# Block-sparse attention and a gated MLP on one core: the output product in one piece, and the end of the kernel in another order

## The chip, the core and the metric

The kernel runs on one core of one Trainium2 chip. That core has a matrix engine (PE in the profile, with its weight loads shown as PEld), three engines for elementwise work (DVE, ACT and POOL) and a queue that mainly issues transfers (SP). They run side by side and wait for each other through semaphores. The metric is the device time of one execution in microseconds (us); lower is better.

## The reference: what is computed

Two stages follow each other. The first is attention over 4 batches, 8 heads, 768 positions and a head size of 64, with a mask made of 32 x 32 blocks (a band of three blocks, the first and last block row and column, and three sampled blocks for each block row). The second is a small MLP over the 3072 rows of 512 that come out of it:

```
scores = scale * q @ k.T ; scores = where(mask, scores, -1e9)
attn   = softmax(scores) ; x = attn @ v            # rows of 512
h      = x @ w_in                                  # 512 -> 1024
solu   = h * softmax(h)
ln     = (solu - mean(solu)) / sqrt(var(solu) + 1e-6) * g_ln
out    = ln @ w_out                                # 1024 -> 512
```

## The kernel before, in words

**Passes and units.** The 24 groups of 128 query rows are taken two at a time, in 12 passes; a pass covers 256 query rows of one batch and all 8 heads. A pass has 12 units (`SLOTS`): 4 pairs of heads times 3 groups of 256 keys. For each unit, `scores` (line 407) issues four matmuls into a PSUM tile `sco`, of which there are two; `exps` (423) is one ACT instruction over 128 x 1024 elements that reads it and so frees it; `outs` (431) issues eight small matmuls into `op`. The unit after next can therefore write its scores only when this unit's `exps` is through. After the third unit of a pair, DVE normalises into the tile `xb`.

**The layer.** Each pass leaves two tiles of 128 rows for the MLP, worked on during the next passes, in between the units. Of one tile: a transfer transposes `xb` into `xT`; `h_mms` (482) issues eight matmuls into `h` (one buffer); `e_exp` (491) is one ACT instruction, `e`, with the row sums; `solu` (499) is one DVE product, after which `h` is free; `ln_turn` sends `solu` through a transposing transfer into `lnT`; `stats` (516) and `rstd` (524) are two and three DVE instructions and a small one on POOL; `o_mms` (542) issues eight matmuls from `lnT` into `o`; `scaled` (550) multiplies by `rstd`, and `store` sends the result out. The softmax's sum and the mean are folded into the statistics and into centred weights `w_cen_sb`.

**What sets the order.** The order is written out by hand. `at(when, fn, ...)` puts a step into a list with a due time in units; `emit` (293) sorts the list by due time and calls the steps, so each engine gets its instructions in this order, and nothing is reordered later. `layer` (815) enters one tile's steps with the due times that its callers give; the tiles of the passes 0 to 9 go through it, twenty in all. For them the eight matmuls of `o` stand in two places: seven at 0.84 of a unit, the eighth at 1.83, which is behind the next unit's four score matmuls (due at 0.8 of each unit) and, for the last of the twenty, also behind the sixteen `outs` matmuls that follow these there. The next tile's first two `h` matmuls come right after the eighth.

**The end.** The last two passes are entered apart. The last pass's first three quarters of `xT` come by transfers; its last quarter is transposed on PE by `x_last` (858) and copied by ACT. `h_end` (868) issues the last two tiles' `h` matmuls into score buffers (`he` in the profile), in four steps over `c`, for two halves each. From `end` on, a list (line 943 on) gives the order: `e_exp`, `solu`, `stats` and `rstd` of the two last tiles (pass `LP`) and of the tile before them; the second tile's `o` of the pass before (`o_mms` with `LP - 1, 1`, whose `lnT` comes by a transfer); PE transposes `ln_mm` (879) into `ln_tp`, copied to `lnTe` by ACT (`ln_out`, 887); `o` of the first last tile (`oe`); and `o` of the second last tile in two halves (`o_half`, `oe1a` and `oe1b`), scaled by DVE and by ACT (`scale_half`), each half with a store of its own.

**The flags.** `check_r`, `check_e`, `check_sum` and `check_bad` (925 to 939) test on DVE that the sums of the softmaxes are in range, add up the flags (`n_ok`), compare the sum (`bad`), and bring the result through a one-column matmul into `bad_i`. All engines read `bad_i` and branch on it; with every flag set, as here, they go on to the end.

Of the kernel before, what the change touches and what calls it, by code (L numbers as in the profile page):

```python
# [208 lines left out]
def kernel(  # L209
# [24 lines left out]
    KD = d_model // 128  # L234
    KF = d_ff // 128
# [6 lines left out]
    PC = 2  # L242
# [5 lines left out]
    SLOTS = NP * UP  # L248
# [6 lines left out]
    n_r, n_e = NPASS * NP * 4, n_tiles  # L255
# [28 lines left out]
    p_op = work.enter_context(tc.tile_pool(name="p_op", bufs=1, space=bass.MemoryType.PSUM))  # L284
# [5 lines left out]
    def at(when, fn, *args):  # L290
        plan.append((when, len(plan), fn, args))

    def emit():
        for _, _, fn, args in sorted(plan, key=lambda x: x[:2]):
            fn(*args)
        plan.clear()
# [98 lines left out]
    def unit(s):  # L395
        ps, r = divmod(s, SLOTS)
        pr, u = divmod(r, UP)
        b, j = divmod(ps, NPB)
        return ps, b, j, pr, u
# [174 lines left out]
    with tc.manual_schedule():  # L574
# [198 lines left out]
        for s in range(n_units):  # L773
            ps, b, j, pr, u = unit(s)
# [37 lines left out]
                at(t0 + t_s, shift, b, pr, key, PC if pr == NP - 1 else 0)  # L812


        def layer(ps, i, hs, es, os):
            for when, n0, n1 in hs:
                at(when, h_mms, ps, i, n0, n1)
            at(es, e_exp, ps, i)
            head = ps == 0 and i == 0
            at(es + (0.33 if head else 0.5), solu, ps, i)  # L820
            at(es + 0.55, ln_turn, ps, i)
            at(es + (6.6 if head else 3.4 if ps == 0 else 2.45 if i == 0 else 1.7), stats, ps, i)
            at(es + (6.7 if head else 3.5), rstd, ps, i)
            for when, n0, n1 in os:
                at(when, o_mms, ps, i, n0, n1)
            out_at = 29.87 if head else os[-1][0] + 0.1
            at(out_at, scaled, ps, i, nc.vector)
            at(out_at + (2.2 if i == PC - 1 and ps < NPASS - 3 else 0.02), store, ps, i)

        LP = NPASS - 1  # L830
        for ps in range(LP):
            b0 = SLOTS * (ps + 1)
            if ps == 0:
                at(b0 + 2.4, x_first, ps)
            else:
                at(b0 - 0.1, x_turn, ps, 0, KD)
            if ps == LP - 1:
                break
            for i in range(PC):
                hs = b0 + 6 * i  # L840
                os = hs + (12 if ps == LP - 2 and i == PC - 1 else 14)
                layer(ps, i,
                      [(hs + 3.9, 0, 2), (hs + 4.85, 2, 3), (hs + 5.86, 3, 5), (hs + 6.85, 5, 7),
                       (hs + (7.79 if hs == SLOTS else 7.85), 7, 8)], hs + 8.5, [(os + 0.84, 0, 7), (os + 1.83, 7, 8)])


        ps, b0 = LP - 1, SLOTS * LP
# [67 lines left out]
        def tile_in(pool, tag, name):  # L915
            if pool is p_sco:
                return lambda: p_sco.tile([128, 2, HF], FP32, tag=tag, name=name)[:, 0, :]
            return lambda: pool.tile([128, d_model], FP32, tag=tag, name=name)
# [11 lines left out]

        def check_sum():
            nc.vector.reduce_sum(out=n_ok[:, 0:1], in_=okr, axis=AX.X)
            nc.vector.tensor_scalar(out=bad, in0=n_ok[:, 0:1], scalar1=float(n_r + n_e),
                                    scalar2=None, op0=ALU.is_lt)

        def check_bad():
            bad_ps = p_h.tile([1, 1], FP32, tag="h", name="bad_ps")
            nc.tensor.matmul(bad_ps, bad, ones_c, start=True, stop=True)
            nc.vector.tensor_copy(out=bad_i, in_=bad_ps)

        end = SLOTS * NPASS
        A, V = nc.scalar, nc.vector
        for n, (fn, *args) in enumerate((
            (h_end, 0, 2, KD),
            (e_exp, LP, 0),
            (o_mms, LP - 1, 0, 5, 8),
            (scaled, LP - 1, 0, A),
            (store, LP - 1, 0),
            (stats, LP - 1, 1),
            (rstd, LP - 1, 1),  # L950
            (check_r, n_r - 2 * PC, n_r),
            (h_end, 1, 0, KD),
            (solu, LP, 0),
            (stats, LP, 0),
            (e_exp, LP, 1),
            (o_mms, LP - 1, 1, 0, 3, tile_in(p_op, "op", "o_10")),
            (ln_mm, 0),
            (ln_out, 0, A),
            (o_mms, LP - 1, 1, 3, 8),
            (solu, LP, 1),  # L960
            (rstd, LP, 0),
            (stats, LP, 1),
            (o_mms, LP, 0, 0, 2, tile_in(p_sco, "sco", "oe0")),
            (ln_mm, 1),
            (ln_out, 1, A),
            (rstd, LP, 1),
            (check_e,),
            (o_mms, LP, 0, 2, 8),
            (scaled, LP - 1, 1, A),
            (store, LP - 1, 1),  # L970
            (scaled, LP, 0, A),
            (store, LP, 0),
            (o_half, 0, p_sco, "sco"),
            (o_half, 1, p_op, "op"),
            (scale_half, 0, V, nc.sync),
            (check_sum,),
            (check_bad,),
            (scale_half, 1, A, nc.scalar),
        )):
            at(end + 0.01 * n, fn, *args)  # L980
# [3 lines left out]
        at(end - 1.12, h_end, 0, 0, 2, (1,))  # L984
        at(end - 1.0, x_last)
        at(end - 1.9, check_r, 0, n_r - 2 * PC)
        at(end - 1.05, o_mms, LP - 1, 0, 0, 3)
        at(end - 0.95, o_mms, LP - 1, 0, 3, 5)
        emit()

    work.close()
# [32 lines left out]
```

## Time and profile before

| what | value |
|---|---|
| time, median of 3 runs | 208.02 us (207.55 to 208.16) |
| the profiled execution's own time | 208.32 us |
| its span, first to last instruction | 206.8 us |
| PE busy over the span | 199.0 us |
| ACT busy over the span | 175.2 us |
| DVE busy over the span | 141.1 us |
| granted PE clock | 1.00 throughout |

All numbers of the trace come from one execution. Times within it count from the span's start. A row of the timeline gives the start, the length, the engine, the line, the operation, output<-input, the shape and the number of like instructions merged into it; brackets give the idle time of that engine ahead of it and what ended it. Matmuls overlap: a row of 512 columns lasts 0.38 us, but the next one starts some 0.215 us after it, so a stop of PE shorter than the difference does not show as idle time.

### The profile page before, as it was taken

Reading aid. Unit: us, or ns where it says so; the run is one execution under the profiler, and the core shown is the slowest. Engines: PE = TensorE matmul, PEld = TensorE weight load, DVE = VectorE, ACT = ScalarE, POOL = GpSimd, SP = SyncE. Lnnn points to the kernel's source line nnn. Section 1 sums busy time; section 2 is a strip of 40 time slices with the busy share of each in tenths; the row PEclk is TensorE's granted clock in tenths of the full one; section 3 lists DMA queues with packets and bytes.
Section 4 is the critical chain, followed back from the end, with each engine's and each line's share of the span. In section 5 each row is a group of like instructions: output and inputs, shape, how many; then the busy total and the mean of one; then the engine's idle time right before and its main releaser. Section 6 shows DMA issues by size and latency. Waiting matters only on the chain.

```text
span 206.8 us, 5603 instructions
## 1 busy us (share of the span) xinstructions
PE 199.0 (96%) x2204; PEld 138.8 (67%) x2238; DVE 141.1 (68%) x331; ACT 175.2 (85%) x209; POOL 110.2 (53%) x167
## 2 busy tenths in 40 slices
PE   7999999999999999999999999999999999999992
PEld 2679967676676676676676676676676676667451
DVE  5688888988755765765665666655665656677982
ACT  6799979889889889889889889879889889897471
POOL 7966799696868274478286273559281110111120
PEclk9999999999999999999999999999999999999999
DMA  5999999979999879999999889999872484556314
GB/s 158 334 367 229 361 373 271 229 134 248 235 264 346 203 168 335 212 153 220 175 232 294 204 161 338 166 241 193 166 196 51 101 105 50 107 125 111 59 50 162
DMA packets 73906, 42.02 MB, mean 203 GB/s; under 512 B 55828, under 2 KB 69396, under 8 KB 73876
## 3 DMA queue, kind: packets, MB, share of 16 engines
q1 hardware_dynamic: 72932, 40.06, 84.1%
q0 software_dynamic: 528, 1.05, 2.7%
q10 hardware_dynamic: 416, 0.52, 0.8%
q8 instruction: 18, 0.29, 0.6%
q14 instruction: 12, 0.10, 0.1%
HBM read 23.07 MB, written 6.29 MB: 142 GB/s over the span
## 4 chain that ended last, share of the span: by engine, by line
PE 90%; DMA 4%; DVE 3%; issue 1%; DVEq 0%
PE sco L416 30%; PE op L444 18%; PE o L547 17%; PE h L487 16%; DMA xT<-xb 3%; PE warm_t L403 2%; DMA lnT<-solu 1%; PE tp_k L346 1%; PE oe L547 1%; PE mean_ps L753 1%; PE tp_q L356 1%; PE he L873 1%; DVE KT L371 1%; DVE QT L664 1%; PE ln_tp L883 0%
## 5 line engine op out<-in xcount | busy, mean ns | idle before, releaser
L427 ACT ACTIVATE exs<-sco 128x1024 bf16<-128x1024 f32 x144 | 141.0, 1024 | 10.3 <-PE sco L416 7.7
L416 PE MATMUL sco<-QT,KT 88*128 88x256 bf16 x576 | 87.4, 274 | 0.3
L416 PEld LDWEIGHTS <-KT 88*128 88x128 bf16 x576 | 54.8, 98 | 31.6 <-issue 4.7
L444 PE MATMUL op<-VA,exs 128*128 128x65 bf16 x1152 | 51.8, 194 | 0.5
L444 PEld LDWEIGHTS <-exs 128*128 128x128 bf16 x1152 | 48.5, 97 | 3.7 <-DVE xb L458 0.3
L487 PE MATMUL h<-w_in_sb,xT 128*128 128x512 bf16 x153 | 48.7, 378 | 0.7
L547 PE MATMUL o<-w_cen_sb,lnT 128*128 128x512 bf16 x166 | 43.3, 379 | 1.0 <-DMA lnT<-solu 0.4
L540 POOL TENSOR_TENSOR rstd<-vpe,mhalf 128x1 f32<-128x1 f32 x24 | 13.2, 549 | 45.4 <-DVE vpe L538 38.9
L457 DVE RECIPROCAL recip_all<-op 128x4 f32<-128x4 f32 x48 | 8.7, 181 | 39.7 <-PE op L444 39.5
L327 POOL COPY KT<-pd 64x768 bf16<-64x768 bf16 (+2 forms) x30 | 21.2, 706 | 23.9 <-DMA pd<-nat 22.8
L496 ACT ACTIVATE e<-h 128x1024 bf16<-128x1024 f32 x22 | 22.5, 1023 | 10.7 <-PE h L487 10.6
L522 DVE BATCH_NORM_STATS2 stats<-solu 128x6 f32<-128x512 bf16 x48 | 30.6, 680 | 0.1
L508 DVE TENSOR_TENSOR solu<-h,e 128x1024 bf16<-128x1024 f32 x22 | 26.7, 1215 | 1.5 <-ACT e L496 1.5
L547 PEld LDWEIGHTS <-lnT 128*128 128x128 bf16 x176 | 15.8, 98 | 14.2 <-DMA lnT<-solu 0.9
L558 DVE TENSOR_SCALAR ot<-o,rstd 128x512 f32<-128x512 f32 x20 | 15.0, 751 | 10.8 <-issue 8.2
L327 POOL COPY QT<-pd 64x768 bf16<-64x768 bf16 (+2 forms) x30 | 20.8, 694 | 1.5
L458 DVE TENSOR_TENSOR xb<-op,recip_all 128x256 bf16<-128x256 f32 x48 | 20.4, 424 | 1.7
L327 POOL CAST nat<-st_q 128x768 bf16<-128x768 f32 (+2 forms) x19 | 13.6, 713 | 14.3 <-DMA st_q<-in_q_dram 14.3
L487 PEld LDWEIGHTS <-xT 128*128 128x128 bf16 x176 | 16.1, 98 | 4.7 <-DMA xT<-xb 0.8
L327 POOL CAST VA<-st_v 128x768 bf16<-128x768 f32 x16 | 13.4, 847 | 1.4 <-DMA st_v<-in_v_dram 0.9
L327 POOL CAST nat<-st_k 128x768 bf16<-128x768 f32 x15 | 12.4, 826 | 3.3 <-DMA st_k<-in_k_dram 3.1
L538 DVE TENSOR_TENSOR vpe<-es,mv 128x1 f32<-128x1 f32 x24 | 6.7, 278 | 0.9
(89 smaller groups left out, 116.5 us busy)
## 6 DMA issues: line engine op xcount, KB each, us to landing
st_v<-in_v_dram SPq DMA_DIRECT2D x16, 384.0 KB, 5.9
out_dram<-ot SPq DMA_DIRECT2D x23, 256.0 KB, 2.8
st_k<-in_k_dram SPq DMA_DIRECT2D x15, 384.0 KB, 5.8
st_q<-in_q_dram SPq DMA_DIRECT2D x12, 384.0 KB, 7.9
w_out_f<-in_moe_w_out_dram SPq DMA_DIRECT2D x4, 512.0 KB, 7.4
st_q<-in_q_dram SPq DMA_DIRECT2D x4, 256.0 KB, 7.9
w_in_sb<-in_moe_w_in_dram POOLq DMA_DIRECT2D x1, 1024.0 KB, 12.0
st_q<-in_q_dram SPq DMA_DIRECT2D x4, 128.0 KB, 4.4
```

The lines of the kernel that those rows point to most:

```text
L327: eng.tensor_copy(out=o, in_=i)
L416: nc.tensor.matmul(sco[:, hh, kk * QW : (kk + 1) * QW], KT[b % 2][0:KR, h * NCH + 2 * u + kk, :], QT[b % 2][0:KR, h * NCH + PC * j : h * N ...
L427: nc.scalar.activation(out=exs_of[ps, pr][:, u].rearrange("p a b c -> p (a b c)"), in_=sco_of.pop(s).rearrange("p a b -> p (a b)"), func=A ...
L444: nc.tensor.matmul(op[:, hh, ic, :], exs[:, u, hh, kk, ic * TQ : (ic + 1) * TQ], VA[b % 2][:, 2 * pr + hh, 2 * u + kk, :], start=(u == 0 a ...
L458: nc.vector.tensor_tensor(out=xb_of[ps][:, pr].rearrange("p c (h d) -> p h c d", h=2), in0=op[:, :, :, 0:D], in1=recip.broadcast_to([TQ, 2 ...
L487: nc.tensor.matmul(h_of[ps, i][:, half, :], xT_of[ps][:, c * PC + i, :], w_in_sb[:, c, half * HF : (half + 1) * HF], start=(c == 0), stop= ...
L496: nc.scalar.activation(out=o, in_=h, func=ACT.Exp, scale=1.0, accum_out=esum_all[:, t : t + 1])
L508: nc.vector.tensor_mul(out=so, in0=h, in1=e)
L522: nc.vector.bn_stats(out=stat_of[ps, i][:, half, :], in_=so[:, half, :])
L540: nc.gpsimd.tensor_tensor(out=rstd_of[ps, i], in0=vpe, in1=mhalf, op=ALU.pow)
L547: nc.tensor.matmul(ops_of[ps, i], lnT_of[ps, i][:, c, :], w_cen_sb[:, c, :], start=(c == 0), stop=(c == KF - 1), skip_group_check=True)
L558: nc.vector.tensor_scalar(out=o, in0=i_, scalar1=r, scalar2=None, op0=ALU.mult)
```

## The change

Four things change. In `layer`, the eight matmuls of `o` are issued in one piece where seven stood; the due time of `scaled` and `store` stays as it was. At the end, the `h` matmuls of both last tiles go ahead of most of the matmuls of `o` of the tile (`LP - 1`, 0), and their two `e` on ACT follow each other directly; of `o` of the tile (`LP - 1`, 1), all eight stand in one piece behind the first transposes. The statistics of the first last tile (`stats`, `LP`, 0) move behind the second `solu`. Of the flags, the last part of `check_r` moves from ahead of the first `solu` to behind the last `rstd`, and the adding-up (`check_sum`) moves ahead of the last tile's scaling, while the comparison stays behind it, in `check_bad`. No instruction is added or taken away: each engine issues as many as before, and POOL and SP issue theirs in the same order.

```diff
--- before.py
+++ after.py
@@ -812,7 +812,7 @@
                 at(t0 + t_s, shift, b, pr, key, PC if pr == NP - 1 else 0)
 
 
-        def layer(ps, i, hs, es, os):
+        def layer(ps, i, hs, es, o_at):
             for when, n0, n1 in hs:
                 at(when, h_mms, ps, i, n0, n1)
             at(es, e_exp, ps, i)
@@ -821,9 +821,8 @@
             at(es + 0.55, ln_turn, ps, i)
             at(es + (6.6 if head else 3.4 if ps == 0 else 2.45 if i == 0 else 1.7), stats, ps, i)
             at(es + (6.7 if head else 3.5), rstd, ps, i)
-            for when, n0, n1 in os:
-                at(when, o_mms, ps, i, n0, n1)
-            out_at = 29.87 if head else os[-1][0] + 0.1
+            at(o_at, o_mms, ps, i, 0, KF)
+            out_at = 29.87 if head else o_at + 1.09
             at(out_at, scaled, ps, i, nc.vector)
             at(out_at + (2.2 if i == PC - 1 and ps < NPASS - 3 else 0.02), store, ps, i)
 
@@ -841,7 +840,7 @@
                 os = hs + (12 if ps == LP - 2 and i == PC - 1 else 14)
                 layer(ps, i,
                       [(hs + 3.9, 0, 2), (hs + 4.85, 2, 3), (hs + 5.86, 3, 5), (hs + 6.85, 5, 7),
-                       (hs + (7.79 if hs == SLOTS else 7.85), 7, 8)], hs + 8.5, [(os + 0.84, 0, 7), (os + 1.83, 7, 8)])
+                       (hs + (7.79 if hs == SLOTS else 7.85), 7, 8)], hs + 8.5, os + 0.84)
 
 
         ps, b0 = LP - 1, SLOTS * LP
@@ -930,10 +929,11 @@
 
         def check_sum():
             nc.vector.reduce_sum(out=n_ok[:, 0:1], in_=okr, axis=AX.X)
+
+        def check_bad():
             nc.vector.tensor_scalar(out=bad, in0=n_ok[:, 0:1], scalar1=float(n_r + n_e),
                                     scalar2=None, op0=ALU.is_lt)
 
-        def check_bad():
             bad_ps = p_h.tile([1, 1], FP32, tag="h", name="bad_ps")
             nc.tensor.matmul(bad_ps, bad, ones_c, start=True, stop=True)
             nc.vector.tensor_copy(out=bad_i, in_=bad_ps)
@@ -941,30 +941,30 @@
         end = SLOTS * NPASS
         A, V = nc.scalar, nc.vector
         for n, (fn, *args) in enumerate((
-            (h_end, 0, 2, KD),
+            (h_end, 0, KD - 1, KD),
             (e_exp, LP, 0),
-            (o_mms, LP - 1, 0, 5, 8),
+            (h_end, 1, 0, KD),
+            (stats, LP - 1, 1),
+            (solu, LP, 0),
+            (rstd, LP - 1, 1),
+            (e_exp, LP, 1),
+            (o_mms, LP - 1, 0, 3, 8),
+            (ln_mm, 0),
+            (ln_out, 0, A),
             (scaled, LP - 1, 0, A),
             (store, LP - 1, 0),
-            (stats, LP - 1, 1),
-            (rstd, LP - 1, 1),
-            (check_r, n_r - 2 * PC, n_r),
-            (h_end, 1, 0, KD),
-            (solu, LP, 0),
+            (solu, LP, 1),
+            (o_mms, LP - 1, 1, 0, 8, tile_in(p_op, "op", "o_10")),
             (stats, LP, 0),
-            (e_exp, LP, 1),
-            (o_mms, LP - 1, 1, 0, 3, tile_in(p_op, "op", "o_10")),
-            (ln_mm, 0),
-            (ln_out, 0, A),
-            (o_mms, LP - 1, 1, 3, 8),
-            (solu, LP, 1),
             (rstd, LP, 0),
             (stats, LP, 1),
             (o_mms, LP, 0, 0, 2, tile_in(p_sco, "sco", "oe0")),
             (ln_mm, 1),
             (ln_out, 1, A),
             (rstd, LP, 1),
+            (check_r, n_r - 2 * PC, n_r),
             (check_e,),
+            (check_sum,),
             (o_mms, LP, 0, 2, 8),
             (scaled, LP - 1, 1, A),
             (store, LP - 1, 1),
@@ -973,7 +973,6 @@
             (o_half, 0, p_sco, "sco"),
             (o_half, 1, p_op, "op"),
             (scale_half, 0, V, nc.sync),
-            (check_sum,),
             (check_bad,),
             (scale_half, 1, A, nc.scalar),
         )):
@@ -984,8 +983,9 @@
         at(end - 1.12, h_end, 0, 0, 2, (1,))
         at(end - 1.0, x_last)
         at(end - 1.9, check_r, 0, n_r - 2 * PC)
-        at(end - 1.05, o_mms, LP - 1, 0, 0, 3)
-        at(end - 0.95, o_mms, LP - 1, 0, 3, 5)
+        at(end - 1.05, o_mms, LP - 1, 0, 0, 2)
+        at(end - 0.95, o_mms, LP - 1, 0, 2, 3)
+        at(end - 0.94, h_end, 0, 2, KD - 1)
         emit()
 
     work.close()
```

## The prediction

> **What bounds the kernel now.** I read the page's busy table and groups first, then the timeline of one layer in the middle, then its first and last counterpart, then the last 17 us. From the page:
>
> ```profile
> span 206.8 us, 5603 instructions
> PE 199.0 (96%) x2204; PEld 138.8 (67%) x2238; DVE 141.1 (68%) x331; ACT 175.2 (85%) x209; POOL 110.2 (53%) x167
> L496 ACT ACTIVATE e<-h 128x1024 bf16<-128x1024 f32 x22 | 22.5, 1023 | 10.7 <-PE h L487 10.6
> ```
>
> PE is busy throughout, and ACT waits for it: 10.6 us in all ahead of `e`. But PE's busy share hides short stops. One layer from the timeline:
>
> ```profile
> 155.00 1.02 ACT L496 ACTIVATE e<-h 128x1024 bf16<-128x1024 f32 x1 [0.57 <-PE h L487]
> 155.49 1.67 PE L547 MATMUL o<-w_cen_sb,lnT 128*128 128x512 bf16 x7
> 156.01 2.84 ACT L427 ACTIVATE exs<-sco 128x1024 bf16<-128x1024 f32 x3
> 156.25 1.22 DVE L508 TENSOR_TENSOR solu<-h,e 128x1024 bf16<-128x1024 f32 x1
> 157.08 0.60 PE L416 MATMUL sco<-QT,KT 88*128 88x256 bf16 x4
> 157.08 0.31 PEld L416 LDWEIGHTS <-KT 88*128 88x128 bf16 x3 [0.19 <-issue]
> 157.51 0.38 PE L547 MATMUL o<-w_cen_sb,lnT 128*128 128x512 bf16 x1
> 157.73 0.59 PE L487 MATMUL h<-w_in_sb,xT 128*128 128x512 bf16 x2
> 158.16 0.49 PE L416 MATMUL sco<-QT,KT 88*128 88x256 bf16 x3
> ```
>
> Seven `o` matmuls last 1.67, one 0.38, so they start (1.67 - 0.38) / 6 = 0.215 apart, and PE is free for the scores at 155.49 + 7 x 0.215 = 157.00. The scores start at 157.08. The first of the three `exs` ends at 156.01 + 1.02 = 157.03: the scores wait for their buffer, which that exponential frees. PE stands still for 0.08 us, hidden under the 0.38 us shown for the last `o`, and the eighth `o`, which needs nothing more, is queued behind the waiting scores. The weight loads show the stop as 0.19 or 0.20 of "issue". It recurs from the first such layer to the last:
>
> ```profile
> 47.20 1.67 PE L547 MATMUL o<-w_cen_sb,lnT 128*128 128x512 bf16 x7
> 48.78 0.31 PEld L416 LDWEIGHTS <-KT 88*128 88x128 bf16 x3 [0.20 <-issue]
> 180.10 0.31 PEld L416 LDWEIGHTS <-KT 88*128 88x128 bf16 x3 [0.20 <-issue]
> ```
>
> At the first, 48.78 - (47.20 + 7 x 0.215) = 0.075. Of the twenty layers 17 have it. The other three are the first (`o` starts late), one whose `lnT` lands late (132.43, below), and the last, where the scores are not held up.
>
> **Part 1, `o` in one piece.** Removed: the stop. The eighth `o` starts at 157.00, the scores at 157.215, past the release at 157.08: nothing is left of it, with 0.13 in reserve. Per layer PE gains 0.075 to 0.08, so 17 x 0.077 = 1.3 us, if nobody else is late next. Behind the moved matmul I look at each in turn.
>
> The `h` pair, by the same spacing, moves to 157.65; it needs `solu`, which ends at 156.25 + 1.22 = 157.47 and releases the weight load 0.05 later. Free. The scores after it move from 158.16 to 158.08; they need the second `exs`, which ends at 156.01 + (2.84 - 1.02)/2 + 1.02 = 157.94: reserve 0.14 less the release, some 0.1. Free, but the tightest. The third `exs` started at 157.82 and now needs scores that end at 157.215 + 0.60 = 157.815: at most 0.05 late, and ACT waits 0.57 for `h` ahead of the next `e`, so the lag dies there. DVE's `scaled` keeps its place and finds `o` done earlier; the store's place in SP's queue is unchanged. No DMA is added.
>
> What can eat some of it is transfers that already land late:
>
> ```profile
> 57.27 0.11 PEld L487 LDWEIGHTS <-xT 128*128 128x128 bf16 x2 [0.29 <-DMA xT<-xb]
> 132.43 1.46 PE L547 MATMUL o<-w_cen_sb,lnT 128*128 128x512 bf16 x6 [0.40 <-DMA lnT<-solu]
> 134.64 0.11 PEld L487 LDWEIGHTS <-xT 128*128 128x128 bf16 x2 [0.49 <-DMA xT<-xb]
> ```
>
> A PE that arrives 0.08 sooner waits 0.08 longer at each of these three, unless their landing moves too. That is 0.24 at most lost, so part 1 lies between -1.3 and -1.06; I take -1.1, near the smaller gain, since the trace does not tell whether these landings follow PE.
>
> **Part 2, the end.** Its rows:
>
> ```profile
> 191.69 0.81 PE L547 MATMUL o<-w_cen_sb,lnT 128*128 128x512 bf16 x3
> 192.34 0.28 PE L861 MATMUL x_tp<-ident,xb 128*128 128x128 bf16 x2
> 192.65 0.37 ACT L864 COPY xT<-x_tp 128x256 bf16<-128x256 bf16 x1 [1.00 <-PE x_tp L861]
> 193.94 1.02 ACT L496 ACTIVATE e<-he 128x1024 bf16<-128x1024 f32 x1 [0.92 <-PE he L873]
> 195.19 1.22 DVE L508 TENSOR_TENSOR solu<-he,e 128x1024 bf16<-128x1024 f32 x1
> 196.32 1.02 ACT L496 ACTIVATE e<-he 128x1024 bf16<-128x1024 f32 x1 [0.68 <-PE he L873]
> 196.40 0.33 PEld L547 LDWEIGHTS <-lnT 128*128 128x128 bf16 x3 [0.61 <-DMA lnT<-solu]
> 197.06 0.61 PE L883 MATMUL ln_tp<-ident,solu 128*128 128x128 bf16 x8
> 197.65 1.21 DVE L508 TENSOR_TENSOR solu<-he,e 128x1024 bf16<-128x1024 f32 x1
> 198.77 0.21 DVE L529 TENSOR_SCALAR es<-esum_all 128x1 f32<-128x1 f32 x1
> 199.20 1.28 DVE L522 BATCH_NORM_STATS2 stats<-solu 128x6 f32<-128x512 bf16 x2
> 199.87 1.01 ACT L325 COPY lnTe<-ln_tp 128x1024 bf16<-128x1024 bf16 x1 [1.14 <-PE ln_tp L883]
> 200.91 0.17 DVE L921 TENSOR_SCALAR okr<-esum_all 128x24 f32<-128x24 f32 x1
> 200.96 1.04 PE L899 MATMUL oe1a<-w_cen_sb,lnTe 128*128 128x256 bf16 x8
> 202.09 0.48 DVE L911 TENSOR_SCALAR ot_last<-oe1a,rstd 128x256 f32<-128x256 f32 x1 [0.80 <-PE oe1a L899]
> 202.49 0.37 DVE L932 TENSOR_REDUCE n_ok<-okr 128x1 f32<-128x216 f32 x1
> 202.90 0.15 DVE L933 TENSOR_SCALAR bad<-n_ok 128x1 f32<-128x1 f32 x1
> 202.96 0.47 ACT L908 ACTIVATE ot_last<-oe1b,rstd 128x256 f32<-128x256 f32 x1 [0.91 <-issue]
> 203.42 0.15 DVE L939 CAST bad_i<-bad_ps 1x1 int32<-1x1 f32 x1 [0.37 <-PE bad_ps L938]
> ```
>
> All in times of before. PE's path: two `o` instead of three stand ahead of `x_tp`, which comes some 0.17 earlier (its `xb` is then the limit), and so does the copy, which ends at 192.85. One `o` and four `he` follow, two `o` fewer than before; the last `he` ends 0.38 sooner, and the first `e` starts at 193.56. The second tile's eight `he` follow without three `o` in between: 0.38 + 3 x 0.215 = 1.03 sooner, `e` at 195.29. The five `o` then run to 196.17; the first `solu` has ended by then (0.23 behind its `e`, as at 156.25, and so by 193.56 + 1.02 + 0.23 + 1.22 = 196.03), so `ln_tp` starts at 196.17 in place of 197.06, and the first `lnTe` copy at 196.82. The eight `o` in one piece start at 196.62, with `lnT` landed by 196.40: the 0.61 of idle weight loads is now filled, with 0.2 to spare. Then two `oe` to 198.78, and the second `ln_tp`, done at 199.39; its copy starts at 199.43 in place of 199.87. All of ACT's and PE's chain behind it is 0.44 earlier: `oe1a` at 200.52, the last ACT scaling at 202.52.
>
> What ACT puts off, the scaling of tile (`LP - 1`, 0), goes between the two copies, where ACT waits 1.14 now; its store goes out later on SP, with only later stores behind it.
>
> DVE's path: the second `solu` follows its `e` by 0.2, at 196.5, 1.15 earlier than before; but the first tile's statistics, which ran while DVE waited for that `e`, now come behind it. Instructions overlap by some 0.08 (`es` starts at 198.77, and the `solu` ahead of it ends at 197.65 + 1.21 = 198.86), so two statistics take 1.28 - 0.08 = 1.20 to their `es`, and `es` to the next step takes 199.20 - 198.77 = 0.43. So: 196.5 + 1.21 - 0.08 = 197.63 statistics, 198.83 `es`, 199.26 statistics, 200.46 `es`, and 200.9 to 200.95 flags, against 200.91. That is the timetable of before: DVE had the time in hand, since it idled 0.80 for `oe1a`. Into this go the moved flags: the two instructions of `check_r`, some 0.3 (twice 0.17 less overlap), `check_e` some 0.4, `n_ok` some 0.3. Scaling starts at about 201.95, not at `oe1a`'s end of 201.56: DVE is the next to be late, by 0.4. Still it is 0.15 ahead of 202.09, and `bad` now follows it directly, without the 0.40 from `n_ok` (202.49) to `bad` (202.90): 0.15 + 0.40 = 0.55 earlier.
>
> The kernel closes after the later of `bad_i` (0.55 earlier) and ACT's last store (0.44 earlier): part 2 is -0.44 to -0.55, and I take -0.5. The moved `rstd` of tile (`LP - 1`, 1) costs nothing: its scaling on ACT comes only behind the second copy. One page of the Trainium skill speaks against this part: "VectorE: DVE Perf Modes", § The DRAIN you can't avoid, has each DVE operation followed by a flush of its duration less 266 ns before the next. By it the two statistics moved behind `solu` would cost 2 x 0.41 more there, and part 2 would come to about +0.2. The rows disagree: `es` starts before `solu` has ended.
>
> **Sum.** -1.1 - 0.5 = -1.6. The profiled execution took 208.32 (1.5 around its span), 0.3 above the median; against the median, 208.02 - 1.6 = 206.4 us, or 206.7 by the profiled one's base.
>
> **The rivals.**
> A. ACT, not PE, sets the pace of the middle: then the gain of part 1 comes back as waits for `exs` a few steps on, and only part 2 is left: 207.5. For it: three `exs` follow each other without a gap, and the next scores have some 0.1 in hand. Against: the 0.57 of ACT's idle time ahead of each `e`. The Trainium skill's "Perfetto Trace Analysis", § Identifying the Most-Contended Engine, would have it so: it takes PE's busy share for no measure, weight loads (67% here) in its place, and occupancy for ACT (85%). 10%.
> B. The middle gains, the end does not: DVE's lengthened queue, or an `lnT` that lands after 196.62, takes part 2 back, between 0 and +0.5: 206.9 to 207.4. For it: DVE is shown above to be the last to come. 13%.
> C. Slower: the scores come 0.13 later behind the longer `o`, and this lag goes round through `exs`, instead of dying at `e`. 17 x 0.13 = 2.2, less part 2: 209.7. It decides if the lag exceeds the 0.57 at `e`; the rows give 0.05. 8%.
> D. The change does nothing that counts: transfers hold PE in the middle (as at 132.43 and 134.64) and closing work hides the end: 208.0. 6%.
> My forecast: 63%.
>
> **Numbers.** Some 0.3%, 0.6 us, is what a measurement of this kernel can tell (its three runs spread over 0.61). The forecast, B and a little of A (which lies at the border, -0.25%) are faster: 0.78. The rest of A and most of D are the same: 0.12. C and the rest of D are slower: 0.10. The range 205.8 to 207.6 holds the forecast, B and A; the forecast's own is 205.8 to 206.9, from all stops gone with 0.6 at the end to three more late landings.
>
> **What would show it.** Right: `sco` rows directly after `o` x8 with no 0.20 "issue" on their weight loads; a layer 0.08 shorter; the last two `e` 1.7 apart, and `ot_last` on DVE waiting for nothing on PE. Wrong: "issue" or ACT waits ahead of the scores that follow the `h` pair (A, C), more time on transposed transfers (D), or a `bad_i` later than 0.4 ahead of before, counted from the tile's last `xb` (B).

## The result, and the profile after

The changed kernel took 206.16 us in the median of six runs (205.58 to 206.53), beside 208.09 for six runs of the kernel before on the same chip: 1.9 us faster by the medians, 1.7 by the ratio of 0.9919 (95% interval 0.9896 to 0.9942, so 1.2 to 2.2 us). The forecast was 206.4. The profiled execution took 205.58, its span 203.94; before it was 208.32 and 206.84.

The page of the changed kernel: the busy shares have hardly moved, and ACT still waits for `h` as long as before.

```profile
PE 195.9 (96%) x2204; PEld 137.3 (67%) x2238; DVE 141.3 (69%) x331; ACT 173.9 (85%) x209; POOL 110.3 (54%) x167
L496 ACT ACTIVATE e<-h 128x1024 bf16<-128x1024 f32 x22 | 22.5, 1023 | 10.7 <-PE h L487 10.6
```

What did move is one row of the groups (line, engine, operation, busy time, mean ns, idle time before it and what ended it): the weight loads of the scores. Before:

```profile
L416 PEld LDWEIGHTS <-KT 88*128 88x128 bf16 x576 | 54.8, 98 | 31.6 <-issue 4.7 <-POOL VA L327 0.7 <-DVE QT L664 0.5
```

After:

```profile
L416 PEld LDWEIGHTS <-KT 88*128 88x128 bf16 x576 | 53.9, 97 | 30.6 <-issue 1.4 <-POOL VA L327 0.7 <-DVE KT L327 0.7
```

The "issue" fell from 4.7 to 1.4 us. In the timeline of the layer that the prediction showed (start, duration, engine, line, operation):

```profile
152.85 1.02 ACT L496 ACTIVATE e<-h 128x1024 bf16<-128x1024 f32 x1 [0.57 <-PE h L487]
153.34 1.89 PE L547 MATMUL o<-w_cen_sb,lnT 128*128 128x512 bf16 x8
153.86 3.80 ACT L427 ACTIVATE exs<-sco 128x1024 bf16<-128x1024 f32 x4
154.85 0.53 PEld L416 LDWEIGHTS <-KT 88*128 88x128 bf16 x4
155.06 0.60 PE L416 MATMUL sco<-QT,KT 88*128 88x256 bf16 x4
155.50 0.60 PE L487 MATMUL h<-w_in_sb,xT 128*128 128x512 bf16 x2
```

Eight `o` from 153.34 at 0.215 end at 155.06, where the scores start; their weight loads wait for nothing. The `h` pair and the next scores (155.94) follow at their spacing (155.50 + 2 x 0.215 = 155.93), four `exs` run without a gap, and `e` still has 0.57 to wait for `h`.

The end of the changed kernel, from the timeline:

```profile
191.12 1.02 ACT L496 ACTIVATE e<-he 128x1024 bf16<-128x1024 f32 x1 [0.71 <-PE he L872]
192.27 1.22 DVE L508 TENSOR_TENSOR solu<-he,e 128x1024 bf16<-128x1024 f32 x1 [0.15 <-ACT e L496]
192.85 1.02 ACT L496 ACTIVATE e<-he 128x1024 bf16<-128x1024 f32 x1 [0.61 <-PE he L872]
193.73 0.61 PE L882 MATMUL ln_tp<-ident,solu 128*128 128x128 bf16 x8
193.76 0.16 DVE L538 TENSOR_TENSOR vpe<-es,mv 128x1 f32<-128x1 f32 x1
193.99 1.23 DVE L508 TENSOR_TENSOR solu<-he,e 128x1024 bf16<-128x1024 f32 x1
195.13 1.28 DVE L522 BATCH_NORM_STATS2 stats<-solu 128x6 f32<-128x512 bf16 x2
198.07 1.04 PE L898 MATMUL oe1a<-w_cen_sb,lnTe 128*128 128x256 bf16 x8
199.17 0.38 DVE L931 TENSOR_REDUCE n_ok<-okr 128x1 f32<-128x216 f32 x1
199.47 0.47 DVE L910 TENSOR_SCALAR ot_last<-oe1a,rstd 128x256 f32<-128x256 f32 x1
199.86 0.14 DVE L934 TENSOR_SCALAR bad<-n_ok 128x1 f32<-128x1 f32 x1
200.07 0.47 ACT L907 ACTIVATE ot_last<-oe1b,rstd 128x256 f32<-128x256 f32 x1 [0.91 <-POOL rstd L540]
200.37 0.14 DVE L939 CAST bad_i<-bad_ps 1x1 int32<-1x1 f32 x1 [0.37 <-PE bad_ps L938]
```

The two last `e` are 1.73 apart, and `ot_last` on DVE waits for nothing on PE: `oe1a` ended at 199.11, DVE came at 199.47. ACT's last scaling starts 0.08 behind the end of `oe1b` (198.95 + 1.04 = 199.99); its row names POOL's `rstd`, which was done 0.8 earlier.

What follows `bad_i` are the engines' reads of it. SP's, before and after, from the view of this tile (line, engine, operation, number; shortest, median and longest in ns; first and last start):

```profile
L992 SPq TENSOR_LOAD <-bad_i x1: 464/464/464, 203.6 to 203.6; - x1
L992 SPq TENSOR_LOAD <-bad_i x1: 612/612/612, 200.5 to 200.5; - x1
```

In all thirteen traces the span ends 2.94 to 2.98 us behind the start of `bad_i`, not counting the length of this read. From the issue of ACT's last store to the end it is anything from 3.22 to 3.46. So it is SP's reading of `bad_i` that the end follows, not ACT's store. `bad_i` came 0.61 earlier, the read took 0.15 longer, and 0.46 is left.

**Where the 2.90 us between the two spans lie.** Executions of one kernel differ in the first 40 us, where the code is the same, so I measure between fixed points: the first weight load of `o` of the third tile, of the nineteenth, and of the twenty-first, which is tile (`LP - 1`, 0). Weight loads of the changed kernel:

```profile
54.18 1.43 PEld L547 LDWEIGHTS <-lnT 128*128 128x128 bf16 x8
176.11 1.43 PEld L547 LDWEIGHTS <-lnT 128*128 128x128 bf16 x8
189.04 0.31 PEld L547 LDWEIGHTS <-lnT 128*128 128x128 bf16 x2
```

The same before:

```profile
54.94 1.21 PEld L547 LDWEIGHTS <-lnT 128*128 128x128 bf16 x7
178.48 1.21 PEld L547 LDWEIGHTS <-lnT 128*128 128x128 bf16 x7
191.48 0.53 PEld L547 LDWEIGHTS <-lnT 128*128 128x128 bf16 x3
```

So 0.76 was there at the third tile, 1.61 came in the sixteen layers up to the nineteenth (123.54 against 121.93), 0.07 in the next two (13.00 against 12.93), and 0.46 behind it (15.36 against 14.90). Not all of the 1.61 is the change: the late `lnT` and `xT` at 132.43 and 134.64 of the profile before are missing here and in the other traces of this study (the one with the changed end alone waits 0.20 for that `xT`, and its layer is no longer than the others). The experiments tell the shares.

### The profile page after: what moved, and what is told of

Read it like the earlier page. It is cut to its first block, busy times and chain, and to the rows that moved or that the text cites. A ratio compares the mean times of both kernels' runs of the same rounds, so it can differ in the third digit from the quotient of the medians.

```text
span 203.9 us, 5603 instructions
## 1 busy us (share of the span) xinstructions
PE 195.9 (96%) x2204; PEld 137.3 (67%) x2238; DVE 141.3 (69%) x331; ACT 173.9 (85%) x209; POOL 110.3 (54%) x167
## 3 DMA queue, kind: packets, MB, share of 16 engines
q0 software_dynamic: 528, 1.05, 2.7%
## 4 chain that ended last, share of the span: by engine, by line
PE 80%; DVE 7%; DMA 4%; POOL 4%; issue 2%; SPq 1%; ACT 0%; DVEq 0%; POOLq 0%
PE sco L416 28%; PE op L444 17%; PE h L487 16%; PE o L547 15%; DMA st_k<-in_k_dram 2%; DVE stats L522 2%; DVE solu L508 2%; DMA lnT<-solu 1%; POOL nat L327 1%; PE mean_ps L753 1%; PE he L872 1%; DVE KT L664 1%; SPq L318 1%; DVE xb L458 1%; DVE vpe L538 1%
## 5 line engine op out<-in xcount | busy, mean ns | idle before, releaser
L416 PEld LDWEIGHTS <-KT 88*128 88x128 bf16 x576 | 53.9, 97 | 30.6 <-issue 1.4
L547 PE MATMUL o<-w_cen_sb,lnT 128*128 128x512 bf16 x166 | 39.9, 379 | 0.5
```

The costliest lines, as they stand in the source:

```text
L416: nc.tensor.matmul(sco[:, hh, kk * QW : (kk + 1) * QW], KT[b % 2][0:KR, h * NCH + 2 * u + kk, :], QT[b % 2][0:KR, h * NCH + PC * j : h * N ...
L547: nc.tensor.matmul(ops_of[ps, i], lnT_of[ps, i][:, c, :], w_cen_sb[:, c, :], start=(c == 0), stop=(c == KF - 1), skip_group_check=True)
```

## The experiments

The table gives, beside the times, the same three distances. "Before" is the median of the kernel before on the same chip.

| kernel | us | before | ratio (95%) | 3rd to 19th `o` | 19th to 21st | 21st to end |
|---|---|---|---|---|---|---|
| before (profile) | | | | 123.54 | 13.00 | 15.36 |
| changed (profile) | 206.16 | 208.09 | 0.9919 (0.9896 to 0.9942) | 121.93 | 12.93 | 14.90 |
| `o` in one piece alone | 206.87 | 207.82 | 0.9962 (0.9940 to 0.9985) | 122.02 | 12.92 | 15.41 |
| the end alone | 207.53 | 207.82 | 0.9988 (0.9959 to 1.0017) | 122.90 | 13.00 | 14.92 |
| `o` as six and two | 211.76 | 207.82 | 1.0206 (1.0156 to 1.0255) | 126.35 | 13.22 | 15.41 |
| one more on ACT | 206.10 | 207.82 | 0.9931 (0.9902 to 0.9959) | 121.82 | 12.92 | 14.92 |
| changed, again | 205.77 | 207.67 | 0.9894 (0.9857 to 0.9931) | 121.89 | 12.93 | 14.90 |
| statistics first | 205.82 | 207.67 | 0.9912 (0.9875 to 0.9948) | 121.85 | 12.93 | 14.75 |
| sum of the flags back | 205.99 | 207.67 | 0.9913 (0.9879 to 0.9947) | 121.87 | 12.93 | 15.00 |
| first `ot` later | 205.84 | 207.67 | 0.9886 (0.9833 to 0.9939) | 121.83 | 12.93 | 14.90 |
| first `rstd` earlier | 204.98 | 207.85 | 0.9856 (0.9815 to 0.9898) | 121.92 | 12.92 | 14.92 |
| that and statistics first | 204.78 | 207.85 | 0.9870 (0.9820 to 0.9920) | 121.99 | 12.92 | 14.77 |
| both, half of the scaling on ACT | 205.03 | 207.85 | 0.9854 (0.9813 to 0.9895) | 121.93 | 12.93 | 14.77 |

### Each part alone

`o` in one piece, with the end of before:

```diff
-                       (hs + ...), 7, 8)], hs + 8.5, [(os + 0.84, 0, 7), (os + 1.83, 7, 8)])
+                       (hs + ...), 7, 8)], hs + 8.5, os + 0.84)
```

> The kernel before with `o` in one piece in every layer, and its own end. My theory (the eighth `o` fills a stop of PE of 0.075 to 0.08 us in 17 layers): 1.1 to 1.3 us faster than before, and the 0.19 to 0.20 of "issue" gone from the weight loads of the scores behind `o`. Rival A (ACT sets the pace) and rival D (nothing counts): within 0.3 us of before. Rival C (the lag goes round): 2.2 us slower. If the 1.9 us between the two kernels came mostly from the end, this run is less than 0.6 us faster.

The changed end, with `o` in seven and one:

```diff
-                       (hs + ...), 7, 8)], hs + 8.5, os + 0.84)
+                       (hs + ...), 7, 8)], hs + 8.5, [(os + 0.84, 0, 7), (os + 1.83, 7, 8)])
```

> The kernel before with the changed end alone, `o` still as seven and one. My theory: 0.4 to 0.6 us faster than before, the first weight load of the last `he` group to the end of the span shorter by that much. Rival B (DVE's lengthened queue or a late `lnT` takes it back): between 0 and 0.5 us slower. If the parts add, the gains of this run and of the one with `o` in one piece together come to the 1.9 us of the whole change, within 0.5.

By the times the first is 0.8 us faster (by the ratio; 0.3 to 1.2), the second 0.25 (from 0.85 faster to 0.35 slower), which by the times alone can't be told from nothing. The fixed points are sharper. Weight loads of `o`, in one piece alone:

```profile
55.29 0.78 PEld L547 LDWEIGHTS <-lnT 128*128 128x128 bf16 x5
177.31 1.43 PEld L547 LDWEIGHTS <-lnT 128*128 128x128 bf16 x8
190.23 0.53 PEld L547 LDWEIGHTS <-lnT 128*128 128x128 bf16 x3
```

and with the changed end alone:

```profile
55.10 0.99 PEld L547 LDWEIGHTS <-lnT 128*128 128x128 bf16 x6
178.00 1.21 PEld L547 LDWEIGHTS <-lnT 128*128 128x128 bf16 x7
191.00 0.31 PEld L547 LDWEIGHTS <-lnT 128*128 128x128 bf16 x2
```

With the end alone, whose middle is that of before, the sixteen layers took 122.90, not 123.54: 0.64 of the profile before belongs to that one execution, most of it to the two late transfers. Against 122.90, `o` in one piece gains 0.88 to 0.97 there, and 0.08 in the next two layers: 1.0 us in all, a little less than the 1.1 to 1.3 expected. The end takes 15.36 to 15.41 with the old order (three traces) and 14.90 to 14.92 with the new (six): 0.46 between the first pair. The parts add, 1.0 + 0.46 = 1.5. Rivals A, C and D of the middle are out, and so is B.

### The stop made larger

```diff
-            [(os + 0.84, 0, 7), (os + 1.83, 7, 8)]
+            [(os + 0.84, 0, 6), (os + 1.83, 6, 8)]
```

> The kernel before with `o` as six and two in place of seven and one, nothing else. My theory: PE then stands still for 0.075 + 0.215 = 0.29 us per layer ahead of the scores, with one more `o` queued behind the waiting scores, so 17 x 0.215 = 3.7 us slower than before, and "issue" of 0.41 on the scores' weight loads. Rival (what the change removes is the cost of breaking off `o`, whatever is left for later): within 0.3 us of before. Rival D (PE is not what sets the pace of the middle): within 0.6 us of before.

4.3 us slower by the ratio (3.2 to 5.3). The layer in the timeline:

```profile
157.14 1.46 PE L547 MATMUL o<-w_cen_sb,lnT 128*128 128x512 bf16 x6
158.73 0.31 PEld L416 LDWEIGHTS <-KT 88*128 88x128 bf16 x3 [0.41 <-issue]
```

"Issue" is 0.41 as worked out ahead, in all layers but the first and the last, and sixteen of them take 126.35 - 122.90 = 3.45 longer, 0.216 each: one matmul of `o`. With the 0.22 of the next two layers that is 3.67, of 3.7 expected. So it is the place of the wait in PE's queue that costs, not breaking off `o`. What of `o` stands behind the waiting scores is paid for in full, until the scores' buffer is free by the time PE gets there.

### Does ACT set the pace?

```diff
+        if ps < NPASS - 1:
+            nc.scalar.activation(out=more, in_=ident, func=ACT.Copy, scale=1.0)
         nc.scalar.activation(out=o, in_=h, func=ACT.Exp, scale=1.0,
```

> The changed kernel with one more instruction on ACT ahead of each `e` of the 22 ordinary tiles (a copy of the 128x128 identity, some 0.25 to 0.3 us, used by nobody). My theory (PE sets the pace, and ACT has 0.57 us of idle time there): within 0.4 us of the changed kernel, so still 1.5 us or more faster than before, and the idle time ahead of `e` down from 10.6 us to about 4. Rival A (ACT sets the pace once the stop is gone): 20 x 0.28 = 5.6 us slower than the changed kernel. If the reserve of 0.1 us of the scores behind the `h` pair is used up in turn: between the two, 1 to 3 us slower.

Its groups on ACT:

```profile
L499 ACT ACTIVATE e<-h 128x1024 bf16<-128x1024 f32 x22 | 22.5, 1022 | 6.8 <-PE h L488 6.8
L498 ACT ACTIVATE more<-ident 128x128 bf16<-128x128 bf16 x22 | 6.7, 306 | 0.0
```

ACT was busy 6.7 us more, and the sixteen layers took 121.82, no longer than without. The wait ahead of `e` fell by 3.8, to 6.8 and not to the 4 expected: instructions on ACT overlap (in the layer at 152 the copy starts at 152.22, 0.09 before the `exs` ahead of it ends, and takes 0.20 of the idle time for its 0.30). Either number is far above the 0 that was paid, so rival A falls. The Trainium skill's rule in "Perfetto Trace Analysis", § Identifying the Most-Contended Engine, which judges PE by its weight loads (67% here) rather than by its 96%, so that ACT's 85% would count for more, does not hold for this kernel.

### What the end is made of

The order on DVE:

```diff
+            (stats, LP, 0),
             (solu, LP, 1),
             (o_mms, LP - 1, 1, 0, 8, tile_in(p_op, "op", "o_10")),
-            (stats, LP, 0),
```

> The changed kernel with the statistics of the last but one tile back ahead of the second `solu`. DVE is busy without a break from 190.8 to 199.9 in the changed kernel, so their place adds nothing to its sum: the second `solu` ends 1.2 later, at about 196.3, just when PE comes to the second `ln_tp` (196.3). Expected: from the last layer's `o` to the end of the span within 0.2 of the 14.9 us of the changed kernel, the second `ln_tp` 0 to 0.15 later. If the order of DVE's work is what made part 2, it goes back towards 15.4.

```profile
193.91 0.16 DVE L538 TENSOR_TENSOR vpe<-es,mv 128x1 f32<-128x1 f32 x1
193.99 1.28 DVE L522 BATCH_NORM_STATS2 stats<-solu 128x6 f32<-128x512 bf16 x2
199.84 0.14 DVE L934 TENSOR_SCALAR bad<-n_ok 128x1 f32<-128x1 f32 x1
```

The end was expected within 0.2, from DVE being busy without a break. It came 0.15 sooner: `bad` comes 10.65 us after the twenty-first `o` (189.19), against 10.82. In the changed kernel the second `solu` starts 0.12 after its `e` (192.85 + 1.02 = 193.87), as the first one does, whose row names ACT; so DVE does stand there, and the expectation was wrong in that: 0.23 from `vpe` (193.76) to `solu`, where it is 0.08 from `vpe` to the statistics in this run. With the statistics ahead this hole is filled. Taken alone, "statistics behind the second solu" therefore costs 0.15 to 0.17. PE's second `ln_tp` stands 7.29 after the twenty-first `o` in both. That the order on PE is what brings the gain follows by elimination, with the sum of the flags (next); neither PE's order nor the new place of `check_r` was changed alone.

The sum of the flags:

```diff
             (check_e,),
-            (check_sum,),
 ...
             (scale_half, 0, V, nc.sync),
+            (check_sum,),
             (check_bad,),
```

> The changed kernel with the sum of the flags back behind DVE's last scaling. By the prediction's step (0.40 from `n_ok` to `bad` saved): `ot_last` on DVE 0.3 earlier, at the end of `oe1a`, `bad` 0.1 to 0.15 later, `bad_i` as much, and the span 0 to 0.15 longer than the changed kernel's, counted from the last layer's `o`. Rival: `bad_ps` waits for PE's `oe1b` anyway, and nothing moves (within 0.05).

```profile
200.02 0.48 DVE L910 TENSOR_SCALAR ot_last<-oe1a,rstd 128x256 f32<-128x256 f32 x1
200.42 0.37 DVE L931 TENSOR_REDUCE n_ok<-okr 128x1 f32<-128x216 f32 x1
200.82 0.15 DVE L934 TENSOR_SCALAR bad<-n_ok 128x1 f32<-128x1 f32 x1
```

`ot_last` comes 0.19 earlier (10.24 after the twenty-first `o`, against 10.43), `bad` and `bad_i` 0.22 and 0.23 later, the end 0.10 later. The rival, by which nothing moves, falls. The moved sum is worth 0.22 at `bad`: it hides the 0.40 from `n_ok` to `bad` behind the scaling, but puts 0.2 in front of it. Of this 0.1 is left at the end, since SP's read of `bad_i` takes 0.46 in this run, as before the change, and 0.61 in the changed kernel.

### The changed kernel again, and a lead that is lost

> The changed kernel itself again, beside the others. By the two terms read from fixed points of the traces (0.065 to 0.075 us per layer in 16 layers, 0.46 at the end) it is 1.5 to 1.7 us faster than before; if the whole were more than its two parts, as the first result of 1.9 us beside 0.8 and 0.3 for the parts alone could mean, it is 1.9 or more. Its first `o` starts anywhere from 37.9 to 39.9 us; from the last layer's `o` to the end of the span it takes 14.9 us.

1.9 us by the medians, 2.2 by the ratio (1.4 to 3.0). The 1.5 of the two parts lies in this interval, so that the times do not show that the whole is more. In the profiled executions what lies beyond the two parts, and beyond the two late transfers, stands ahead of the third tile. In the three traces of before and of each part alone the first `o` starts at 39.45 to 39.91, in all traces of the whole change at 37.8 to 38.7, and for `o` as six and two at 38.25. Part of such a lead is lost again at once. Here PE, DVE and POOL of the changed kernel, each from its timeline:

```profile
48.70 0.11 PEld L487 LDWEIGHTS <-xT 128*128 128x128 bf16 x2 [0.50 <-DVE solu L508]
44.59 0.75 DVE L558 TENSOR_SCALAR ot<-o,rstd 128x512 f32<-128x512 f32 x1 [0.70 <-POOL rstd L540]
47.43 1.22 DVE L508 TENSOR_TENSOR solu<-h,e 128x1024 bf16<-128x1024 f32 x1
43.98 0.57 POOL L540 TENSOR_TENSOR rstd<-vpe,mhalf 128x1 f32<-128x1 f32 x1
```

The first tile's `rstd` stands on POOL behind six copies, the first of which waits 1.41 for a transfer; they run from 38.29 to 43.89. DVE's `ot` waits for it, DVE's `solu` is late behind `ot`, and `h` on PE waits for `solu`. I tried first to move `ot` behind the next statistics:

```diff
-            out_at = 29.87 if head else o_at + 1.09
+            out_at = 29.95 if head else o_at + 1.09
```

> The changed kernel with the scaling of the very first tile (`ot` of layer 0) one place later on DVE, behind the next tile's statistics. In three executions whose first `o` came early (37.94, 38.25 and 38.40) the `h` at 48.7 to 49.0 waited 0.50 to 1.09 for `solu`, and DVE had stood 0.70 to 1.33 for POOL's `rstd` in front of that `ot`; in the three with a first `o` at 39.45 or later there was no such wait. Theory (DVE's order passes POOL's lateness on to PE): `ot` waits for nothing, DVE's `solu` of the third tile is done before `h` needs it, the stop at 48.7 is gone, and an early execution keeps its lead, so 0 to 0.9 us faster than the changed kernel from one execution to another, some 0.3 in the median. Rival (the lead is lost anyway, to the next thing that comes by the loads' timetable): the stop comes back within two layers under another name, and the median is within 0.2 us of the changed kernel.

```profile
46.45 0.75 DVE L558 TENSOR_SCALAR ot<-o,rstd 128x512 f32<-128x512 f32 x1 [1.43 <-POOL rstd L540]
```

It was worse in this trace: `ot` waited 1.43, and the next `o`, which needs the buffer that `ot` frees, 1.05; 205.84 us is no gain. Then I left DVE's order and put `rstd` one place earlier on POOL, by a later due time of the copies ahead of it:

```diff
-            [21.3, 21.4, 26.0, 27.3, 30.1, 30.15, 38.2, 39.0],
+            [21.3, 21.4, 27.25, 27.3, 30.1, 30.15, 38.2, 39.0],
```

> The changed kernel with the first layer's `rstd` one place earlier on POOL, ahead of the third pair of transposed-block copies in place of behind it; DVE's and PE's orders are untouched. Putting DVE's `ot` later did not help, as POOL's `rstd` was then the later one still (46.45). Theory (POOL's queue behind the loads is what makes that `ot` late): `rstd` is done at about 42.7 in place of 44.55, `ot` waits for nothing, and `o` of the third tile comes 15.5 us after that of the first, in place of the 15.7 to 17.0 of the five executions of this order whose first `o` started by 38.7: 0.2 to 0.9 us faster than the changed kernel in the median. Rival (the lead goes to the next late thing): 15.7 or more between these two `o`, and within 0.2 us.

```profile
42.24 0.87 POOL L540 TENSOR_TENSOR rstd<-vpe,mhalf 128x1 f32<-128x1 f32 x1 [0.16 <-DVE vpe L538]
```

`ot` (at 43.80) waits for nothing, and the third tile's `o` comes 15.38 after the first's (53.82 - 38.44); it is 15.39 in each of the two traces that follow, and was 15.71 to 17.04 in the six traces with an early first `o` and with `rstd` and `ot` in their old places. 204.98 us, 2.9 less than before beside it, where the changed kernel was 1.9 less in each of its two comparisons. The intervals of the ratios still overlap (0.9815 to 0.9898, and 0.9857 to 0.9931), so how much it gains is read from the traces: 0.3 to 1.7, by how early the first `o` came and how much of that was lost.

Two more went on from there: the statistics first, and then the first half of the last scaling on ACT, which idles 0.91 there ("the run before" is in each case the kernel just told).

```diff
-            (scale_half, 0, V, nc.sync),
+            (scale_half, 0, A, nc.sync),
```

> The run before with the statistics of the last but one tile back ahead of the second `solu`, which alone took 0.15 to 0.2 us off the end (14.71 from the last layer's `o` to the end, against 14.86 to 14.92). Theory (DVE is the last to be late, and its wait of 0.15 for the second `e` is filled): the end at 14.7, and with the earlier `rstd` 0.4 to 1.0 us faster than the changed kernel. Rival: 14.9, and no faster than the run before.

> The run before with the first half of the last scaling on ACT, which idles 0.91 us there, in place of DVE. Theory (DVE is the last to be late): `bad` 0.3 earlier, `bad_ps` directly behind `oe1b`, `bad_i` and the end 0.1 to 0.16 earlier, 14.55 to 14.6. Rival (ACT's last store sets the end as soon as `bad_i` is earlier): within 0.05 of 14.7.

The first repeats the shorter end (14.77) and gives 204.78; in time it can't be told from the kernel without it. In the second `bad` comes 0.29 earlier, but `bad_i` only 0.07 and the end no sooner: `bad_ps` now waits for the last `oe1b` on PE, and SP's read of `bad_i` takes 0.71 in place of 0.65. The rival was right that nothing is gained. Its reason, ACT's last store, is not shown: the end keeps its distance to the read.

## Why the prediction was right, point by point

**The stop of 0.075 to 0.08 in 17 layers.** The cause was right, and the experiment with six and two shows it from the other side. The size was nearly right too: against the trace with the end alone, fourteen of the sixteen layers are 0.06 to 0.08 shorter (7.67 to 7.68 there, 7.60 to 7.61 here, in most), and the last two layers, of which one has the stop, 0.07. Fifteen stops of 0.07 come to the 1.04 measured. The other two layers gain nothing, by the next point. The earliest stop, at 48.78, belongs to the head's timetable.

**The deduction for late landings.** I took 1.1 instead of 1.3 since PE would wait 0.08 longer at three transfers. The value was right (1.04), and the reason half right. The waits at 132.43 and 134.64 made the profiled execution 0.6 longer and come back in no other trace at that length, which one profile alone does not tell. The one at 57.27 does recur, and the changed kernel has another like it:

```profile
56.44 0.11 PEld L487 LDWEIGHTS <-xT 128*128 128x128 bf16 x2 [0.18 <-DMA xT<-xb]
102.21 0.11 PEld L487 LDWEIGHTS <-xT 128*128 128x128 bf16 x2 [0.20 <-DMA xT<-xb]
```

These stand in the two layers of sixteen that gained nothing (7.67 and 7.70, against 7.68 each with the end alone): PE came earlier and waited. That the deduction came to the right sum, with other transfers than those named, is partly luck.

**What comes next behind the moved matmul.** `h` behind `solu`, the scores with 0.1 in hand, the third `exs` at most 0.05 late: the layer shows all three, and the `exs` not late at all. Rival C had no ground, since nothing went round.

**The end, from the twenty-first `o`.** First `e` 0.38 sooner: 2.46 to 2.08. Second `e` 1.03 sooner: 4.84 to 3.81. `ln_tp` 0.89 sooner: 5.58 to 4.69. `oe1a` 0.44 sooner: 9.48 to 9.03. ACT's last scaling 0.44 sooner: 11.48 to 11.03. DVE's scaling 0.15 ahead of before and about 0.4 behind `oe1a`: 10.61 to 10.43, and 0.36 behind. `bad_i` 0.55 earlier: 11.94 to 11.33, 0.61. The whole is 0.46, between the 0.44 and 0.55 given, but not for the reason given. The prediction let the kernel close after the later of `bad_i` and ACT's last store. The traces show the end at a fixed distance from the read of `bad_i`, and this read took 0.15 longer, a term that the prediction did not have. The read takes 0.46 to 0.47 in the traces in which it starts behind the issue of ACT's last store, and 0.61 to 0.71 in those in which it starts ahead of it; why was not tried. That 0.61 - 0.15 comes to ACT's own 0.45 may be luck; no run settles it. The prediction also did not ask what the statistics' new place costs on DVE: its timetable is right, but with the old place the end is 0.15 sooner.

**The rule of a flush between DVE operations** (the Trainium skill, "VectorE: DVE Perf Modes", § The DRAIN you can't avoid) would by the prediction's estimate have made the end 0.2 slower (0.82 less the 0.55 gained is nearer to 0.3). The section itself adds that a next operation that is not held starts earlier, and the rows agree with that. In the new order too the statistics (195.13) start before the `solu` ahead of them has ended (193.99 + 1.23 = 195.22), and the end was 0.46 faster.

**The sum.** 1.5 us is what the fixed points give, 1.6 was the forecast; the first comparison gave 1.9 by the medians, and the later one 1.9 again; both intervals hold 1.5. In the profiled executions the third tile came earlier too. I had no term for that, and it is not settled whether the change has to do with it, as the code of the first 38 us is the same.

## What to carry to other kernels

A stop shorter than the modelled end of a matmul does not show as idle time of PE; look for it in the weight loads ("issue", the same number in every turn of the loop), and move behind the wait nothing that could run ahead of it. Compare two traces between fixed points inside, not by their ends: here the part of the gain that belongs to the change (1.5) and what may be chance (0.6 of late transfers, 0.8 at the start) were of one size. A small operation on a queue that otherwise follows loads can hold up two other engines; moving it forward was worth 0.3 to 1.7 us in the traces, beside the 0.46 of the whole new order of the end. When one engine of the end is made earlier, follow the chain to the last instruction: here a read of one number took back a quarter of what had been gained.

## What the runs showed that I had not expected

At first PE takes almost twice as long for the same work, and the moment at which it gets faster differs from one execution to the next. The same two 128x512 matmuls of zeros on the start-up path, in the trace before, with the first exponential:

```profile
6.51 1.06 PE L403 MATMUL sco<-zer 128*128 128x512 bf16 x2
8.46 1.02 ACT L427 ACTIVATE exs<-sco 128x1024 bf16<-128x1024 f32 x1 [0.92 <-PE sco L416]
```

and in the trace of the changed kernel:

```profile
5.90 0.59 PE L403 MATMUL sco<-zer 128*128 128x512 bf16 x2
7.24 1.95 ACT L427 ACTIVATE exs<-sco 128x1024 bf16<-128x1024 f32 x2
```

1.06 against 0.59 for the same pair, and the first exponential 1.22 later. The granted clock of the profile is 1.00 in this stretch (4 to 8 us) of both traces, so it does not show this; the lengths of the rows do. Most of the 1.05 by which the first `o` differs is there already. The slow form stands in the traces of before and of each part alone (first exponential 8.46 to 8.92); the others have the first exponential at 7.24 to 8.12. The Trainium skill describes such a thing in "TensorE: Matmul & The Clock Gate", § What's actually happening: half rate until PE has been busy for about 3.4 us, by a window that runs freely and so falls differently from run to run. The traces agree with a rate that rises early in the run, at a moment that varies between executions; that a window's phase is the cause was not tried. Of thirteen profiled executions three had the slow form, and none of the nine with both parts of the change; this may be chance, or not.
